# Attention with packed queries and a two-layer MLP on one Trainium2 core: two more block-product groups, crossbar transposes of queries, idle matmuls, another order

## The chip, the cores and the metric

The kernel runs on one core of a Trainium2 chip. The core has a matrix engine (TensorE, PE in the profile, with its weight loads as PEld), a vector engine (VectorE, DVE), a scalar engine (ScalarE, ACT), GpSimd (POOL) and SyncE (SP). Each engine takes its instructions in order, and waits on semaphores where one needs the result of another. PE writes only to PSUM, from which DVE or ACT copy. DMAs are issued by SP, ACT or POOL and carried out by 16 shared DMA engines. The metric is device time in microseconds; the median of the runs counts.

## What is computed

`q`, `k`, `v` have shape (8, 8, 576, 64): eight batches of eight heads with 576 tokens of 64 numbers. `p` has 32 packed queries for each head. The reference, cut to what matters:

```python
def sm_attn(qq, kk, vv):
    s = scale * np.matmul(qq, kk.transpose(0, 1, 3, 2))       # scale = 1/8
    a = np.exp(s - np.max(s, axis=-1, keepdims=True))
    a = a / (np.sum(a, axis=-1, keepdims=True) + 1e-09)
    return np.matmul(a, vv)
p_packed = sm_attn(p, k, v)            # 32 rows per head
out = sm_attn(q, p_packed, p_packed)   # 576 rows per head, over 32 keys
x = out.transpose(0, 2, 1, 3).reshape(4608, 512)
h = x @ w_in                           # 512 -> 2048
g = np.maximum(h, 0) ** 2
return g @ w_out                       # 2048 -> 512
```

All inputs and the output are float32; the kernel computes in bfloat16 with sums in float32.

## The kernel before

**Tiling.** Work goes by batch. The heads form two quads `qd` of four. For a batch `b`: `tr_k` transposes the keys in 32x32 blocks on DVE, `s1` (L283, L296) multiplies them with the block-diagonal packed queries, `s1_exp` takes the exponential, and `pv` (L316, L320) multiplies with `v` and sums. `extract` copies the result `pp` to SBUF, `recip` takes the reciprocal of the sums, and `pq_block` (L331, casts at L164 and L166) writes `pp` once more as a block-diagonal matrix `pq_bd`. `m` (L354) multiplies `pp` with `w_in` before attention is applied, as 64x32 tiles of the array: the product `M` has 32 rows for each head, 256 in all. `tr_q` (L267) transposes the queries on DVE into the single tile `qT`. `s2` (L379) multiplies `qT` with `pq_bd`, `s2_exp` (L386) takes the exponential, `n_sum`, `n_ln`, `n_inv` and `n_mul` (L391, L396, L399, L405) normalise. `f1_mm` (L417) then multiplies the attention weights with `M`: a piece `fb` of 128 of the 2048 hidden columns is four matmuls of 288 columns into a tile of `ps_h` (two exist). `f1_relu` (L445 on ACT, L447 on DVE) and `f1_sq` (L452, DVE) make the columns of `gT`. Batch 0 (in `SPLIT`) is done in halves (L426, L435, L437); all others are "wide".

**Layer two.** The 4608 tokens are 36 tiles of 128. A tile alone is 16 matmuls of 512 columns (`f2_mm`, L501) into one of the two banks `ps_o` (tiles 2 and 3: `ps_a`), one copy into `o_sb` (three buffers) and a store. Four tiles from each number in `GROUPS` are computed together with seven block products in place of eight (Strassen's scheme in Winograd's form): `w_sum` (L525) makes four sums of blocks of `w_out` once, `g_sum` (L546) makes four sums `wS` of blocks of `gT` for each group in two halves each, `prod` (L560) runs seven products of 16 matmuls of 256 columns, and `prod_out` (L166 or L164, and L573 where it adds) empties a bank after each product, so seven times instead of four. The last tile, 35, is done in two halves of 256 columns (L487).

**Stores.** `store` (L477) issues four DMAs of 32 rows for a tile at the point where its last copy is emitted, all on SP; for the last tile two of each four go to ACT.

**Order.** The schedule is written by hand, with no reordering: each step is cut into pieces with the engines that may do it and a planned time, and `ORDER` (L71) is a compressed list that names, for each piece, its engine and its position. `Plan.run` (L59) emits the pieces in that sequence, and each engine keeps the order in which it got them. The planned times, the number of buffers (`plan.nslots`, L585) and `plan.base` (L859), the planned starting times of engines and DMA, are used for making the list only. Loads are issued by POOL (they convert float32 to bfloat16), at most eight under way (`dl`); the keys of batch 0 come in float32 on SP and ACT (L221).

Of the kernel before, what the change touches and what calls it, by code (L numbers as in the profile page):

```python
# [14 lines left out]
P = 128  # L15
D = 64
NP = 32
QH = 4
# [8 lines left out]
GROUPS = (15, 19, 23, 27, 31)  # L27
SPLIT = (0,)

# [20 lines left out]
class Plan:  # L50

    def __init__(self, slots):
        self.nslots = slots
        self.streams, self.base = [], {}

# [3 lines left out]
    def run(self, order):  # L59
# [5 lines left out]
        for c, p in sorted(zip(code, pieces), key=lambda x: x[0] % 4096):  # L65
            e, us, fn = p.alts[c // 4096]
            self.log.append((p.step.name, p.stage, e, c % 4096, us))
            fn()


ORDER = (  # L71
    'c-jrtgMu9i6a~Pm)5-X86x+6K+qP}nwr$(CZQHhY>nn=LD1aOaqU01vp_H0J$V=%+DJCT*AH}2W<fbUfL>Vb7m7*+^n<`Km%0R^^0VSb=RFq0n'
    'Z7NUIsSCBDj<k@PP#c;-J!v3qp%FBJ4p2>ML_?`QHK*|un-Wr9s!Fw}FO{T<)Qmb%H(E<$X)>LpO|*-i(rQ{y_h=f;p-VKMmeDmjLZ|30U8L)z'
    'e4NhGce+iF$i)xo1;yg$^qvy&JNiN?`78aQtn6VQ7v}_=ge&nsiou20&vCdMXW;BymuqnYp2&H*2)E&;+@4o(DXzdhcmNOQZJdnLaCI)vRk<&Z'
    '<;i@Et8r}}%p-Ul@8w3^lIQSO{>KqAgBS35e!_3~7x(1;ypeqpTT)A2DJ12@CE=1lp7Td0DJJEmp%j$jQd@5E1Afi-`6++m(o#j5$$S3JK~hm_'
    'N_)wm*|mVqmnE`JmdkqCD>=2G*4DMMSq{r$StVQLtNanuESg)(YcVaWEwr3g*S`8spniQI&*ZKA6jqm((n{J%^J#Idr%a$=5{f~Q6o=xw;!;vd'
    'Mk!pmD2!a>p<a}O^3XT>O&z!kAL6UrPiDz=xh=!J<21EpF+YX7V!0wH+BJZ7l5sm0xg>2h5v8I6RD{Y=6{<sHD3lX&J}%4McnR;|ef)z>Qc5<d'
    'ERE!{ypteJuA_9C&eq+U&dOLNTW={TEv2Vyl$ml;KFUvpsIaRHm7wCTQ8bmN&`g?5i|H>3$K(Ka1c$hzxD40eDqN2nb2IMB6L>05<3&81=eh6j'
    'W4^~<_$UA2K=DYVM0v7ELQgz7BuC|l9GBB_R<6iZxhZ!%ujRQslv-L>8)-9btZlTNcGND~%{xMSX>adKeXXzboxayk`dPp0PyOX(3o`PxvbNUF'
    '23kk!W<zYajk57J)28?q`dU&uS9=;p6KOQ<pna}AbeV3@eR8vx<8omx%@z3(zu=edzwAh`#FylfUXIC0&jqQY4ZIDtwYK+m&^|iAJ5WFB7yasO'  # L80
    'W4)|{4YFZ2#-`aUo8x<9@9e#=ELEmTRE=s-U1~^8sU9_^*3_9APz!2Hov15yr+ze;dQfi~LL(_LC*@R}meX+-F2Kb&8|UJpT$$JKdfvcWcsuXr'
    'yX=)~e1ln%NDj#@`K72-kgC#Fx=I)6E(2t!e3EbSTSx;mSUnm`!!$zUX(1h><8`b~)~PyEm*`5JrE_(g9#gMHSbR%jnJt^;vG$hF3Ro$tVH<6;'
    '?Xcap#}3*l`)Nn)m_4u%^r1o2pN7*on&g^J^Jp$DaxJBmw1zg&M%qe8=>#34b98~OxbDysdPcA54Sl4~^pk#(<F3OE-SxSJyDfL(&fJ}QaUbr-'
    'LwFdE<}o~pr|?Xk#mjgxujV~`fDiH!KF+83G@s)Oe3=VNS*a!Uq=7V%rqV*%NGItjeWb4p@(hvTGDgP9B$?`&BGYA_ERqGXLe|Je*(BR!r|gzJ'
    'vR`h=eYq!3<f*)rSMpx|N=)@?Y>lf4yzw=OH<_l?)S6b)X(r94xipU!)}mTk%V=etuM2gNF7+<gRk~W&=?2}bTXeg3r|!|cx?d0K5k0CW^pu{}'
    'b9zxP=~ca^H}$sO*9ZDYpXv+!r|J`PEWm;-(84U-Vq08GV96|vrLv5c--=pED{G~#f>pMvR?TW!ZL4SXt&uIYRleo6+D_VeyI_~?s@<@gcE|49'
    'Q~P1R?U(&C0pK7ef)I)@xZy_x!V%?9h$KjiWd4*$gS5ziOvs9C$ca42k3uMl;wXjED2Ixuf*Poe`e=nlXo~jegpTOr?~Y!WMayYB9j3eViilJ2'
    'Kpx5Cc`a|^GklS6b8G1(qh*53mDRFC4$5cwB|c5BS+%5A)S9|hH|Zfgt(Wz>KGx^zw|JJ&3R)d&Xw9s(U9^Yx+7yBCA|BEqI|`!&YN91NqX&jz'
    '0j;9Vw3|-T8G1=S2pq_f9FLQ8PR`E-xu$ysZKJ)kpAOM2`aqv3h=Vyc$LHLfhf8otZp}+*9UY|ebd_$>1A0u%VI0oUoSM^fCeF+`+)cPSx8jc6'
    'n+New9>vpnF3;zMyp&h+X5Pgo+!^^HXOIF?L`q3rSt$4PjegKS>b7W0ZaJ*8^|Qe?)F#?=TV~sApB=UncFk_tJxhel$c-|njJjxuCYXX*Sb}xf'  # L90
# [13 lines left out]
def kernel_impl(tc, q, k, v, p, w_in, w_out, out):  # L104
# [15 lines left out]
    with ExitStack() as ctx:  # L120
# [38 lines left out]
        def bd(t, h, dh):  # L159
            return both(t, dh * BDW + 32 * h, P + (-32 if h % 2 else 32), 32)[32 * h:32 * h + 32]  # L160
# [524 lines left out]
        def s2_steps(b):  # L685
# [16 lines left out]
            if wide:  # L702
                return [res[0], res[2], res[1], res[3]]
# [228 lines left out]
```

The softmax here doesn't subtract the row's maximum and nothing guards it: scores larger than these inputs give would overflow.

## Time and profile before

| | |
|---|---|
| five runs | 251.13 us median, 249.48 to 252.84 |
| profiled execution | 251.13 us, its span 249.1 us |
| mean granted PE clock | 0.988 |
| matmuls start, end | 7.7 us, about 241.7 us |
| matmuls L501 / L560 / L417 | 240 / 560 / 448 |
| DVE transposes of q (L267) | 18, 21.9 us together |
| HBM read, written | 37.22 MB, 9.44 MB |

The page cuts the span into 40 slices of 6.2 us each. A digit is the busy share in tenths:

```profile
DVE  4875649876788797679787989988897798768410
ACT  3377667985697676776788788887875756400010
POOL 7797556562075003261010000000000000000000
PEclk9999999999799999999999999999999999999997
DMA  6999999999969963799711010033004101504243
GB/s 222 202 183 204 205 201 208 204 246 218 180 79 185 247 137 57 118 167 213 143 45 42 3 42 3 0 75 99 3 21 118 34 3 39 130 2 105 66 108 103
```

Loads fill the DMA engines in the first ten slices and come in lumps until slice 20; what follows is mostly stores. The clock row shows one slice below full, between 62 and 68 us, and the last. In tables of groups a row gives line, engine, operation, output<-inputs, shape and count, busy time and mean duration, then the idle time of the engine just before, with what ended it. In a timeline a row starts with start and length in us; the lengths of matmuls are modelled and overlap, so the pace is read from start to start.

### The profile page before, as it was taken

To read this page: it belongs to the slowest core of one execution; us is meant where nothing else is said; L and a number is where in the kernel's file an instruction comes from. 1 tells how busy PE (TensorE), PEld (TensorE's weight loads), DVE (VectorE), ACT (ScalarE), POOL (GpSimd) and SP (SyncE) were. 2 spreads that over 40 slices of the span, in tenths; PEclk is the share of its full clock that TensorE was granted. 3 is DMA by queue.
4 is the path that set the end of the run, shared out by engine and by line. 5 is a ranking of instruction groups with operands and counts; after the bars stand their busy time and mean duration, and the time that the engine had idled before them with its cause. 6 is when DMAs were issued, how large, how long until landed. Compare 5 with 4: busy or idle time off the path is not lost.

```text
span 249.1 us, 5373 instructions
## 1 busy us (share of the span) xinstructions
PE 227.8 (91%) x2096; PEld 161.3 (65%) x2096; DVE 186.0 (75%) x325; ACT 157.8 (63%) x273; POOL 59.9 (24%) x120
## 2 busy tenths in 40 slices
PE   0669999996999999999999999999999999999980
PEld 0525564573554666666646778887787888888860
DVE  4875649876788797679787989988897798768410
ACT  3377667985697676776788788887875756400010
POOL 7797556562075003261010000000000000000000
PEclk9999999999799999999999999999999999999997
DMA  6999999999969963799711010033004101504243
GB/s 222 202 183 204 205 201 208 204 246 218 180 79 185 247 137 57 118 167 213 143 45 42 3 42 3 0 75 99 3 21 118 34 3 39 130 2 105 66 108 103
DMA packets 27160, 29.01 MB, mean 116 GB/s; under 512 B 5760, under 2 KB 18816, under 8 KB 27136
## 3 DMA queue, kind: packets, MB, share of 16 engines
q0 software_dynamic: 19472, 17.99, 45.6%
q1 hardware_dynamic: 7328, 9.97, 14.7%
q10 hardware_dynamic: 336, 0.72, 0.8%
q8 instruction: 16, 0.26, 0.4%
q14 instruction: 8, 0.07, 0.1%
HBM read 37.22 MB, written 9.44 MB: 187 GB/s over the span
## 4 chain that ended last, share of the span: by engine, by line
PE 70%; DMA 19%; POOL 4%; issue 2%; DVE 1%; SPq 0%; ACT 0%; POOLq 0%
PE ps_o L560 24%; PE ps_h L417 20%; PE ps_o L501 15%; DMA v_r<-in_v_dram 6%; DMA w_in_b<-in_moe_w_in_dram 4%; DMA q_b<-in_q_dram 4%; DMA k_b<-in_k_dram 4%; PE ps_m L354 3%; PE ps_s L379 2%; PE ps_a L283 2%; PE ps_pp L316 1%; PE ps_s L391 1%; DMA out_dram<-o_sb 1%; POOL w_in_b L246 1%; POOL v_r L238 1%
## 5 line engine op out<-in xcount | busy, mean ns | idle before, releaser
L445 ACT ACTIVATE r<-ps_h 128x576 bf16<-128x576 f32 x99 | 63.7, 650 | 27.5 <-PE ps_h L417 25.5
L417 PE MATMUL ps_h<-a,M 128*128 128x288 bf16 x448 | 71.6, 288 | 0.0
L501 PE MATMUL ps_o<-w_out_b,gT 128*128 128x512 bf16 x208 | 59.2, 382 | 0.5 <-DMA w_out_b<-in_moe_w_out_dram 0.5
L417 PEld LDWEIGHTS <-M 128*128 128x128 bf16 x448 | 43.9, 98 | 16.8 <-issue 0.5
L452 DVE TENSOR_TENSOR gT<-r 128x1152 bf16<-128x1152 bf16 x64 | 46.9, 747 | 7.6 <-ACT r L445 5.5
L560 PEld LDWEIGHTS <-wS 128*128 128x128 bf16 x320 | 31.0, 98 | 4.7 <-issue 0.4
L501 PEld LDWEIGHTS <-gT 128*128 128x128 bf16 x240 | 22.6, 99 | 17.0 <-issue 3.4
L560 PE MATMUL ps_o<-wT,wS 128*128 128x256 bf16 x240 | 30.5, 273 | 0.0
L238 POOL DMA_DIRECT2D v_r<-in_v_dram x32 | 19.0, 598 | 35.3 <-DVE wT L525 16.3
L164 ACT CAST M<-ps_m 128x1024 bf16<-128x1024 f32 (+1 forms) x26 | 23.0, 915 | 5.8 <-PE ps_m L354 4.9
L267 DVE STREAM_TRANSPOSE qT<-q_b 128x1152 bf16<-128x1152 bf16 (+1 forms) x18 | 21.9, 1227 | 5.5 <-DMA q_b<-in_q_dram 5.4
L560 PEld LDWEIGHTS <-gT 128*128 128x128 bf16 x240 | 23.3, 98 | 3.8 <-issue 0.4
L164 ACT COPY o_sb<-ps_o 128x512 f32<-128x512 f32 (+1 forms) x15 | 8.6, 572 | 22.7 <-PE ps_o L560 19.6
L560 PE MATMUL ps_o<-w_out_b,gT 128*128 128x256 bf16 x160 | 20.9, 273 | 0.0
L166 DVE COPY o_sb<-ps_o 128x512 f32<-128x512 f32 (+1 forms) x20 | 13.4, 671 | 8.1 <-PE ps_o L560 3.6
L283 PE MATMUL ps_a<-pT_bd,kT 128*128 128x128 bf16 x128 | 10.9, 241 | 8.2 <-DVE kT L273 8.2
L386 ACT ACTIVATE e<-ps_s,rD 128x576 bf16<-128x576 f32 (+1 forms) x18 | 12.2, 687 | 8.0 <-PE ps_s L379 8.0
L166 DVE CAST M<-ps_m 128x1024 bf16<-128x1024 f32 (+1 forms) x10 | 11.2, 1118 | 6.8 <-PE ps_m L354 6.1
L283 PEld LDWEIGHTS <-kT 128*128 128x128 bf16 x128 | 9.2, 109 | 10.8 <-DVE kT L273 8.7
L573 DVE TENSOR_TENSOR o_sb<-ps_o,o_sb 128x512 f32<-128x512 f32 x15 | 10.3, 689 | 6.2 <-PE ps_o L560 5.0
L379 PE MATMUL ps_s<-qT,pq_bd 128*128 128x288 bf16 x64 | 11.6, 306 | 3.3 <-DVE qT L267 2.0
L405 DVE SCALAR_TENSOR_TENSOR a<-e,rD,ls 128x576 bf16<-128x576 bf16 (+1 forms) x18 | 13.3, 740 | 1.5 <-ACT ls L399 1.5
(72 smaller groups left out, 303.7 us busy)
## 6 DMA issues: line engine op xcount, KB each, us to landing
out_dram<-o_sb SPq DMA_DIRECT2D x140, 64.0 KB, 1.7
k_b<-in_k_dram POOLq DMA_DIRECT2D x14, 288.0 KB, 8.7
q_b<-in_q_dram POOLq DMA_DIRECT2D x14, 288.0 KB, 8.7
v_r<-in_v_dram POOLq DMA_DIRECT2D x16, 160.0 KB, 8.5
v_r<-in_v_dram POOLq DMA_DIRECT2D x16, 128.0 KB, 6.9
w_in_b<-in_moe_w_in_dram POOLq DMA_DIRECT2D x8, 256.0 KB, 8.9
w_out_b<-in_moe_w_out_dram POOLq DMA_DIRECT2D x8, 256.0 KB, 8.5
k_f<-in_k_dram ACTq DMA_DIRECT2D x1, 576.0 KB, 4.2
```

What stands on the lines that cost most here:

```text
L164: nc.scalar.copy(dst, src)
L166: eng.tensor_copy(dst, src)
L238: nc.gpsimd.dma_start(self.vr[32 * i:32 * i + 32, h0:h1, :n * D], src[:, :, J0[i] * D:(J0[i] + n) * D])
L267: nc.vector.transpose(self.qT[:, qd, :, j0 * 32:j1 * 32].rearrange("p dh (j a) -> p j dh a", a=32), self.t.qb[qd][:, j0 * D:j1 * D].rearra ...
L283: nc.tensor.matmul(ps[:, g * P:(g + 1) * P], lhsT=self.kT[:, qd, g * P:(g + 1) * P].bitcast(BF16).rearrange("p (t two) -> p two t", two=2) ...
L379: nc.tensor.matmul(ps[:, c], lhsT=self.pq[:, blk(qd, dh)], rhs=self.qT[:, qd, dh, n0:n0 + HALF], start=(dh == 0), stop=(dh == 1))
L405: nc.vector.scalar_tensor_tensor(out=self.a2[:, qd, n0:n1].rearrange("p (c n) -> p c n", n=HALF), in0=self.e2[qd, hf], scalar=self.rD[:, q ...
L417: nc.tensor.matmul(ps[:, c, :HALF], lhsT=a.M[:, qd, fb * FB:(fb + 1) * FB], rhs=a.a2[:, qd, c * HALF:(c + 1) * HALF], start=(qd == 0), sto ...
L445: nc.scalar.activation(dst, src, ACT.Relu)
L452: eng.tensor_tensor(out=gT[:, fb - 1:fb + 1, o:o + S], in0=r, in1=r, op=ALU.mult)
L501: nc.tensor.matmul(po[t], lhsT=gT[:, fb, n0:n0 + P], rhs=w_out_b[:, fb, :], start=(fb == 0), stop=(fb == NFB - 1))
L560: nc.tensor.matmul(ps[:, u * EH:(u + 1) * EH], lhsT=lhs, rhs=rhs, start=(n in (1, 2, 4) and kk == 0 and u == 0), stop=(kk == KB - 1 and u ...
```

## The change

- `GROUPS` gets 7 and 11: tiles 7 to 14 are computed as block products too, seven groups in all.
- `XBAR` names batches 4 to 7. Their `q` is transposed by a DMA issued by SP (`xbar_q`, SBUF to SBUF) instead of by DVE. Pairs of token columns lie in the partitions then, so the rows of those batches come out in another order, and `store` addresses them accordingly. `qT` has two buffers instead of one.
- The block-diagonal `pq_bd` and its two memsets fall away. `s2` runs as small tiles of the array instead: 32 matmuls of 32x32 for a wide batch (16 for each half of batch 0), or 16 matmuls of 64x32 for a batch in `XBAR` (`s2_x`), both quads in one step, which takes both `ps_h` tiles. `pq_part` copies the blocks that lie in the wrong partitions (three small casts in each of two pieces), `pq_swap` does it in two casts for batches in `XBAR`.
- `FILL` and `keep_clock`: ahead of eleven early steps PE runs 97 matmuls in all, of 224 columns, of a zeroed tile; their result is overwritten.
- `f1_sq` may run on ACT; `e1` and `e1r` have one buffer; `e2` has two for each quad instead of three in all.
- Stores are steps of their own, in pieces of two DMAs, on SP, on POOL (from tile 8 on) or on ACT (from tile 31 on).
- `ORDER` is another list, some planned times differ, and `setup_rest` on POOL is shorter by one memset.

The diff, without the list and with less of the planning:

```diff
-GROUPS = (15, 19, 23, 27, 31)
+GROUPS = (7, 11, 15, 19, 23, 27, 31)
 SPLIT = (0,)
+XBAR = (4, 5, 6, 7)
+PQ_PARTS = (((0, 1), (1, 0), (1, 1)), ((2, 0), (2, 1), (3, 0)))
...
+            self.fill = FILL.get(p.step.name, 0) if e == "PE" else 0
...
+FILL = {'S1.0.0': 31, 'S1.0.1': 4, 'PV.0.0': 12, 'M.0.0': 16, 'N.0.0.0': 11, 'S2.0.1': 3, 'N.0.0.1': 10, 'R.0.0': 1, 'R.0.2': 3, 'R.0.1': 4, 'R.0.4': 2}
...
+            nc.vector.memset(idle_b, 0.0)
...
-            nc.vector.memset(pq_bd[0][:, :BDW + 2 * P], 0.0)
...
-            nc.gpsimd.memset(pq_bd[1][:, :BDW + 2 * P], 0.0)
+
+        def keep_clock(ps):
+            for _ in range(plan.fill):
+                nc.tensor.matmul(ps, lhsT=idle_b[:, :P], rhs=idle_b, start=True, stop=True)
...
             def tr_q(self, qd, hf=None):
-                self.tile_of("qT", att, [P, NQD, 2, S], BF16, bufs=1)
+                self.tile_of("qT", att, [P, NQD, 2, S], BF16)
...
+            def xbar_q(self, qd):
+                self.tile_of("qT", att, [P, NQD, 2, S], BF16)
+                nc.sync.dma_start_transpose(self.qT[:, qd].rearrange("p dh s -> p (dh s)").rearrange("p (jp r) -> p jp r", r=P), self.t.qb[qd])
...
             def s1(self, qd):
                 ps = ps_att.tile([P, 512], F32, name="ps_a", tag="a")
+                keep_clock(ps[:, :224])
...
-            def pq_block(self, pr, eng):
+            def pq_part(self, i, eng):
+                self.tile_of("pq", small, [P, NQD, 2, 32], BF16, bufs=2)
                 ps = self.ps_pp if eng is nc.vector else self.pp
-                for e in range(2):
-                    for dh in range(2):
-                        s0 = 64 * e + 32 * dh
-                        cast(eng, bd(self.pq, 2 * pr + e, dh),
-                             both(ps, pr * 64 + 32 * e, P + (-32 if e else 32), 32)[s0:s0 + 32])
+                for h, dh in PQ_PARTS[i]:
+                    pr, e = divmod(h, 2)
+                    s0 = 64 * e + 32 * dh
+                    cast(eng, self.pq[32 * h:32 * h + 32, :, dh], both(ps, pr * 64 + 32 * e, P + (-32 if e else 32), 32)[s0:s0 + 32])
+
+            def pq_swap(self, e, eng):
+                self.tile_of("pq", small, [P, NQD, 2, 32], BF16, bufs=2)
+                ps = self.ps_pp if eng is nc.vector else self.pp
+                s = P + (-32 if e else 32)
+                src = ps[64 * e:64 * e + 64, 32 * e:32 * e + 2 * s].rearrange("p (q c i) -> p q c i", q=2, i=32)[:, :, 0:3:2]
+                cast(eng, self.pq[64 * (1 - e):64 * (1 - e) + 64], src)
+
+            def packed(self, h, qd, dh):
+                pr, e = divmod(h, 2)
+                if e + dh == 2 * pr:
+                    return self.pp[32 * h:32 * h + 32, qd * P + pr * 64 + 32 * (e ^ qd):][:, :32]
+                return self.pq[32 * h:32 * h + 32, qd, dh]
...
-            def s2(self, qd, hf):
-                ps = self.pss[qd, hf] = self.ps_s(hf)
+            def s2_x(self):
+                for qd in range(NQD):
+                    ps = self.pss[qd, None] = ps_h.tile([P, 2, 512], F32, name="ps_s", tag="h")[:, :, :HALF]
+                    qT = self.qT[:, qd].rearrange("p dh s -> p (dh s)").rearrange("p (jp r) -> p jp r", r=P)
+                    for x in range(QH):
+                        h = x ^ qd
+                        pr, e = divmod(h, 2)
+                        for par in range(2):
+                            w = self.pp[:, qd * P + pr * 64 + 32 * (x % 2):][:, :32] if par == e else self.pq[:, qd, pr]
+                            nc.tensor.matmul(ps[32 * x:32 * x + 32, par].rearrange("p (jp a) -> p jp a", a=32), lhsT=w[64 * par:64 * par + 64],
+                                             rhs=qT[64 * par:64 * par + 64, :, 32 * h:32 * h + 32], start=True, stop=True)
+
+            def s2(self, hf):
+                if self.b in XBAR:
+                    return self.s2_x()
+                if hf is None:
+                    pss = [ps_h.tile([P, 2, 512], F32, name="ps_s", tag="h")[:, :, :HALF] for _ in range(NQD)]
+                else:
+                    ps = ps_h.tile([P, 2, 512], F32, name="ps_s", tag="h")
+                    keep_clock(ps[:, 0, :224])
+                    pss = [ps[:, qd:qd + 1, :HALF] for qd in range(NQD)]
                 for c, n0 in enumerate([hf * HALF] if hf is not None else [0, HALF]):
                     for dh in range(2):
-                        nc.tensor.matmul(ps[:, c], lhsT=self.pq[:, blk(qd, dh)],
-                                         rhs=self.qT[:, qd, dh, n0:n0 + HALF],
-                                         start=(dh == 0), stop=(dh == 1))
+                        for h in range(QH):
+                            for qd in range(NQD):
+                                o = 32 * (h ^ qd)
+                                nc.tensor.matmul(pss[qd][o:o + 32, c], lhsT=self.packed(h, qd, dh), rhs=self.qT[32 * h:32 * h + 32, qd, dh, n0:n0 + HALF],
+                                                 start=(dh == 0), stop=(dh == 1))
+                for qd in range(NQD):
+                    self.pss[qd, hf] = pss[qd]
...
-            eng.tensor_tensor(out=gT[:, fb - 1:fb + 1, o:o + S], in0=r, in1=r, op=ALU.mult)
-
-        po, ob = {}, {}
+            dst = gT[:, fb - 1:fb + 1, o:o + S]
+            if eng is nc.scalar:
+                eng.activation(dst, r, ACT.Square)
+            else:
+                eng.tensor_tensor(out=dst, in0=r, in1=r, op=ALU.mult)
...
-        def store(t, src, eng=None, e0=0, e1=NE):
-            for i in range(4):
+        def store(t, src, i0, eng, e0=0, e1=NE):
+            for i in range(i0, i0 + 2):
                 b, j = divmod(t * 4 + i, JT)
+                if b in XBAR:
+                    j = 2 * (j % JH) + j // JH
                 dst = out[b * S:(b + 1) * S, e0:e1].rearrange("(a j) e -> j a e", j=JT)[j]
-                (eng or nc.sync if i % 2 else nc.sync).dma_start(dst, src[32 * i:32 * i + 32])
+                eng.dma_start(dst, src[32 * i:32 * i + 32])
...
-                old = [f"S2.{b - 1}.{qd}.{hf}" for qd, hf in halves(b - 1)]
+                old = [f"S2.{b - 2}.{hf}" for hf in parts(b - 2)] if b > 1 else []
             us = 0.84 if nm == "k" else 1.37
+            if nm == "q" and b in XBAR:
+                return [Step(f"Tq.{b}.{qd}", [stage([("SP", 0.4, lambda qd=qd: T[b].xbar_q(qd))]), stage([("-", 1.2, lambda: None)]),
+                                              stage([("DMA", 2.0, lambda: None)])],
+                             [f"Lq.{b}.{qd}"] + old, (), [("kqb", 2, f"Lq.{b}.{qd}")], lag=0.5) for qd in QDS]
...
+                res.append(Step(f"S2.{b}.{hf}",
+                                [stage([("PE", (0.25 if b else 0.5) * m, lambda hf=hf: T[b].s2(hf))]),
+                                 stage(*[[("ACT", 0.73 if wide else 0.49, lambda qd=qd, hf=hf: T[b].s2_exp(qd, hf))] for qd in QDS])],
+                                [f"XT.{b}/2.{i}" for i in range(3)] + [f"Tq.{b}.{qd}" + (f".{hf}" if b in SPLIT else "") for qd in QDS],
+                                [("h", m), ("e20", 1), ("e21", 1)], [("h", 1, None)]))
...
-                res.append(Step(f"F1.{b}.{fb}", [stage([("DVE", 0.77, lambda fb=fb: f1_sq(T[b], fb, V))])], deps, (),
+                res.append(Step(f"F1.{b}.{fb}", [stage([("DVE", 0.77, lambda fb=fb: f1_sq(T[b], fb, V)), ("ACT", 1.14, lambda fb=fb: f1_sq(T[b], fb, A))])], deps, (),
...
+        def store_step(name, ts, after, slot, hf=None):
+            def piece(t, i):
+                args = (hf * EH, (hf + 1) * EH) if hf is not None else ()
+                return [(e, us, lambda eng=eng: store(t, src[t if hf is None else (t, hf)], i, eng, *args))
+                        for e, us, eng in (("SP", 0.86, nc.sync), ("POOL", 1.0, Q), ("ACT", 0.86, A))
+                        if e == "SP" or t >= (8 if e == "POOL" else 31)]
+            return Step(f"ST.{name}", [stage([("-", 0.0, lambda: None)]), stage(*[piece(t, i) for t in ts for i in (0, 2)]),
+                                       stage([("-", 1.8, lambda: None)])],
+                        [after], (), [("osb", 2, slot)] if slot else [], lag=0.1)
...
-        plan.base.update(DVE=2.7, POOL=1.25, ACT=2.1, ACTQ=0.75, SP=0.7, DMA=1.85, PE=3.6)
+        plan.base.update(DVE=2.5, POOL=1.25, ACT=2.1, ACTQ=0.75, SP=0.7, DMA=3.2, PE=3.6)
...
+        plan.stream(7.5, store_steps())
```

## The prediction

> **What bounds the kernel now.** I read the page first, then windows, then the groups of TensorE (PE) instructions after the last stall, then timelines of the places where PE does not run at full pace, and the stores at the end.
>
> ```profile
> PE 227.8 (91%) x2096; PEld 161.3 (65%) x2096; DVE 186.0 (75%) x325; ACT 157.8 (63%) x273; POOL 59.9 (24%) x120
> ...
> 80.00:140.00 60.00, 60.00 (x502) 37.17 (x501) 48.87 (x82) 44.16 (x72) 11.34 (x24) 1.00 0.66 125
> ...
> 150.00:190.00 40.00, 40.00 (x421) 33.02 (x416) 35.90 (x65) 31.45 (x58) 0.00 (x0) 1.00 0.17 41
> ```
>
> The two window rows give length, then busy us of PE, weight loads, DVE, ACT and POOL, the clock, the DMA share and GB/s. PE has no recorded idle time. Since ends of matmuls are modelled, I counted: the groups after 65.4 us, each at its pace from start to start (0.49 us for 4 matmuls of 288 columns, 0.216 for one of 512, 20.32/186 = 0.109 for one of 256, 0.56 for 16 packed ones), give some 174.5 us of work. The last matmul ends near 241.7, so 176.3 us pass. PE is 99% full for seven tenths of the span: there a microsecond of PE work removed is a microsecond gained, as long as DVE and ACT keep up. They are 82% and 74% busy in 80 to 140, 90% and 79% in 150 to 190.
>
> The places where PE loses time lie before and after that stretch:
>
> ```profile
> 7.69 1.04 PE L283 MATMUL ps_a<-pT_bd,kT 128*128 128x128 bf16 x8 [7.69 <-DVE kT L273]
> ...
> 13.48 1.15 PE L379 MATMUL ps_s<-qT,pq_bd 128*128 128x288 bf16 x4 [1.26 <-ACT pq_bd L164]
> ...
> 47.42 0.61 PE L283 MATMUL ps_a<-pT_bd,kT 128*128 128x128 bf16 x8
> ...
> 59.28 0.38 PE L501 MATMUL ps_o<-w_out_b,gT 128*128 128x512 bf16 x1
> 61.70 0.78 PE L379 MATMUL ps_s<-qT,pq_bd 128*128 128x288 bf16 x4 [2.04 <-DVE qT L267]
> ```
>
> The same eight matmuls of L283 take 1.04 us at 7.69 and 0.61 at 47.42. Until about 24 us everything on PE goes at half pace, though the granted clock of the early slices reads full. At 59.7 PE stands 2.04 us, because the queries of batch 2 landed at 60.24, and then it runs at half clock again: the windows 60 to 65 and 65 to 70 have a mean granted clock of 0.71 and 0.95, which is some 3.4 us at 0.5 and costs 1.7 us more.
>
> ```profile
> 236.00:241.70 5.70, 5.65 (x52) 4.81 (x50) 1.12 (x2) 0.58 (x1) 0.00 (x0) 1.00 0.37 98
> 241.70:249.10 7.40, 0.00 (x0) 0.00 (x0) 0.00 (x0) 0.37 (x1) 0.00 (x0) 0.82 0.39 102
> ...
> L481 SPq DMA_DIRECT2D out_dram<-o_sb x20: 314/421/435, 237.2 to 246.5; - x20
> L481 ACTq DMA_DIRECT2D out_dram<-o_sb x4: 322/389/462, 240.4 to 242.5; - x4
> ```
>
> After the last matmul 7.4 us pass, with one copy of 0.37 us in them. SP issues stores one after another at 0.42 us from 237.2 until 246.5, while ACT's last is issued at 242.5. The end is a backlog of SP's queue.
>
> **The change, part by part.** I sum against the profiled run (251.13 us, span 249.07), which is also the median of the five.
>
> *Two more product groups* (tiles 7 to 14). A group of four tiles is 64 matmuls of L501 or 112 of L560: 64 x 0.216 = 13.8 against 112 x 0.109 = 12.2 us. Twice 1.6 is **-3.2**. On DVE each adds a fifth of the wS work of five groups, (13.6+6.8+6.8)/5 = 5.4 us, and three more evictions at 0.69: 7.5 a group, 15 in all. Eight transposes of 1.37 us leave DVE (-11 in all, some 5.5 before 140) and the block-diagonal casts shrink (from eight of about 0.23 a batch to six, or two larger ones planned at 0.3; about -1 a batch). In 80 to 140 that is 48.9 + 15 - 5.5, over 58 of 60 us. ACT must take some of it: the diff lets it square (planned at 1.14 us, against 0.747 on DVE), and it has 16 us free there. DVE at 90% with ACT at 79% left PE full in 150 to 190; the sum here, (58.4+44.2)/120 = 85%, is the same, but less even. I charge **+3** (0 to +10).
>
> *Packed scores.* S2 was eight matmuls a wide batch, 2 x 0.49 = 0.98 us. Now batches 4 to 7 use 16 on tiles of 64 rows by 32 columns, the others 32 on 32 by 32. The nearest row is the product M:
>
> ```profile
> 73.22 0.41 PE L354 MATMUL ps_m<-w_in_b,pp 64*32 64x512 bf16 x8
> ...
> 73.45 0.40 PE L354 MATMUL ps_m<-w_in_b,pp 64*32 64x512 bf16 x8
> 73.78 0.39 PE L501 MATMUL ps_o<-w_out_b,gT 128*128 128x512 bf16 x1
> ```
>
> Eight run together, eight more 0.23 us later, the next work at 0.56: two rounds of 0.216 and some 0.12 for entering and leaving. So 16 matmuls of 288 columns cost 2 x 0.122 + 0.12 = 0.36 (-0.62), 32 cost 4 x 0.122 + 0.12 = 0.61 (-0.37). A rule speaks against it: the Trainium skill, TensorEngine Tiling (Array Packing), Gotcha 1: PSUM Pressure, says that different row tiles cannot use one PSUM bank at the same time. In the 32-row form four row tiles write one bank; by the rule they go in turn, 16 x 0.122 = 1.95 us, +1.0 a batch instead of -0.37. But in the row above the two row tiles of M write the same bank and start together, so I go by the row; by the rule the sum would be 1.3 us worse, since only batch 3 of that form lies in the full stretch (the 64-row form puts its two row tiles in two banks). A batch's scores now take both ps_h tiles at once, as M does already; F1 then waits for one exp (L386, 0.69 us), which layer-two matmuls cover; without them 0.7 a batch, 3.5 in all. Batches 3 to 7: **-2.9** (+1 to -2.9; a dearer issue of four row tiles, which no row shows, would eat the gain).
>
> *Queries through the crossbar.* Eight transposes of 288 KB on SP's queue. The trace shows none. Nearest rows: a 64 KB store lands in 1.7 us, a 288 KB load among other loads in 8.7; 261 GB/s with a split middle dimension, as the skill has it (DMA: Bandwidth & Descriptors, Latency and other measured facts), would be an estimate of 1.1 us and the latency. I take 4 us each, 1.7 to 9 as the ends. They are hidden: the DVE transposes they replace were done at 85 to 88 (batch 4), 111 to 117 and 132 to 140, and the scores that use them began at 108, 130 and 154, at least 13 us after. Batch 7's second transpose at 179.7 was just in time, but its q was issued at 117.6, and qT now has two buffers. Cost 0. What stands behind a waiting transpose on SP is stores, and behind them three o_sb buffers, then PSUM; SP waits for data most of the time (99 us on one line of its waits), and DMA is a fifth busy after 120.
>
> *Idle matmuls.* 97 of 224 columns. The 31 ahead of the first S1 can start after a first memset, near 1.3 us: 18 at half pace (0.187) and 13 at full (0.093) end near 6, before kT is there at 7.69. The other 66 are 6.1 us at full pace; PE's idle time in 10 to 20 is 2.8 us and grows by the half-pace time saved there, so they fit barely. Half-pace work until 24 us adds up to some 11 us, so at most 5.5 is to be had. From 20 to 59 PE has hardly a gap, so what is won can be carried on, unless weights (landing until 43) hold it: **-3.0** (+4 to -5.5).
>
> *Another order.* The stop at 59.7 to 65.5 cost 3.75 us. The plan now takes loads to land 1.35 us later than it did (DMA base 1.85 to 3.2), so it will put other work into most of it: tiles 4 to 6 are ready by then, as F1 of batch 1 ended at 57.8. **-2.5** (+3, where another step meets its data late, to -3.75). POOL's memset of 0.64 us goes; it stands among load issues, but DMA is full there: 0.
>
> *Stores* become steps of their own, two DMAs each, spread over SP and POOL, for the last tile ACT too. 16 issues of the last group at 0.42 in two queues are out by about 241. Then copy 0.37, two issues 0.84, landing 1.7 from the last issue, and the 0.9 between landing and end as now: 3.5 after the last matmul instead of 7.4. POOL's issues of loads took 0.56 and land slower, so **-3.5** (0 to -3.9).
>
> Sum: -3.2 + 3.0 - 2.9 + 0 - 3.0 - 2.5 - 3.5 = -12.1: **239.0 us**.
>
> **The rivals.**
> *Early gains don't last (B).* Until 61 us loads keep DMA full (205 GB/s in nearly every slice), and their order stays. If the q of batch 2 still decides, a PE that is early only waits longer: the two parts of -5.5 fall away, 244.5. For it: the DMA row; against it: work of tiles 4 to 6 was lying there.
> *DVE becomes the bound in 80 to 140 (C).* Friction of 9 to 12 instead of 3, most of the rest kept: about 248.
> *The clock doesn't answer to idle matmuls (F).* They do not do what they are for: 66 x 0.187 = 12.3 us against gaps of 3 to 8 puts 4 or more onto PE where 3 were to be won: 246.
> *Slower: the crossbar (D).* At S2 of batches 4 to 7 PE's queue waits in order. The pair of a batch has at least 13 us; beyond that each microsecond stops PE four times. The other gains, about 12, are gone when a pair takes 16 us, 8 a transpose; slower by 1% from 17. At 9 us each, the upper end above, 4 x (18-13) = 20 makes 259. Against it: loads of this size need that long only when DMA is full, which it is not after 120.
>
> **How the numbers follow.** Forecast 0.48 (239), B 0.21 (244.5), C 0.12 (248, half of it within 1%), F 0.07 (246), D 0.12 (259). Faster by over 1% (under 248.6; less than that can't be told from no change): 0.48 + 0.21 + 0.07 + 0.06 = 0.82; within 1% 0.06; slower 0.12. The low end takes every gain at its full size and no friction, -19: 232. With B, C and F the range reaches 250; outside lie D, a little of C and of the forecast's low end, under 0.2.
>
> **What would show it.** L283's first group at about 0.6 us; no gap over 1 us and no half clock near 60; L501 at 112 matmuls and L560 at 784; 16 packed score matmuls in under 0.4 us; DVE under 95% in 80 to 140; 3 to 4 us from the last matmul to the end, no SP row past it by 5. I am wrong if PE waits for a DMA-written qT, if PE shows gaps in the middle stretch with DVE as releaser, or if the idle matmuls stand ahead of work whose data are there.

## The result, and the profile after

| | |
|---|---|
| forecast | 239.0 us (232 to 250) |
| before | 250.47 us median of 80 runs |
| after | 248.71 us median of 43 runs, 246.64 to 251.96 |
| ratio after / before | 0.9923, 95% interval 0.9905 to 0.9941 |

The change brings 1.8 to 1.9 us where 12.1 were forecast. Ratios here leave disturbed runs out; medians don't, so the two can differ a little. The profile shown is that of a repeat of the changed kernel (label after_again, 247.92 us, span 246.2); the first one (label after) is of an execution of 250.35 us, above the median, and is used only where it is named. Line numbers of the changed kernel: S1 L296 and L310, packed scores L430 (32x32) and L413 (64x32), idle matmuls L192, F1 L470, a tile alone L561, group products L620, last tile L547, casts and copies L170 (ACT) and L172 (DVE), stores L541. In experiments that add lines of code they are 2 to 9 higher.

The page, and windows in the columns of before (length, then busy us of PE, weight loads, DVE, ACT, POOL, clock, DMA share, GB/s); the last is from the last matmul to the end:

```profile
PE 226.8 (92%) x2407; PEld 173.7 (71%) x2417; DVE 181.1 (74%) x315; ACT 159.0 (65%) x265; POOL 89.0 (36%) x177
...
POOL 8765476618482012094603300240016005004070
PEclk9799999999999999999999999999999999999995
```

```profile
80.00:140.00 60.00, 56.28 (x637) 44.62 (x635) 47.66 (x79) 46.05 (x73) 19.39 (x39) 1.00 0.75 128
150.00:190.00 40.00, 40.00 (x429) 33.00 (x414) 33.05 (x54) 29.39 (x46) 8.25 (x17) 1.00 0.19 49
237.80:246.20 8.40, 0.00 (x0) 0.00 (x0) 0.00 (x0) 0.37 (x1) 0.95 (x2) 0.67 0.17 47
```

PE had 60.00 busy us of 60 in 80 to 140 and now has 56.28: it stands 3.7 us there, while DVE, at 47.66, is no busier than before. The last matmul ends at 237.8 instead of 241.7, so PE is 3.9 us early; but 8.4 us pass after it where 7.4 did. The half clock near 62 to 68 is gone from the clock row, and one slice below full lies at the start, from 6.2 to 12.3 us. POOL, idle after 125 us in before, has stores in slices up to the last but one.

The start of PE's timeline, and later the packed scores:

```profile
1.05 5.09 PE L192 MATMUL ps_a<-idle_b 128*128 128x224 bf16 x31 [1.05 <-DVE idle_b L175]
8.09 0.69 PE L296 MATMUL ps_a<-pT_bd,kT 128*128 128x128 bf16 x8 [1.95 <-DVE kT L285]
...
11.32 1.59 PE L192 MATMUL ps_pp<-idle_b 128*128 128x224 bf16 x12 [0.47 <-ACT e1r L317]
12.74 0.28 PE L331 MATMUL ps_pp<-e,v_b 128*128 128x64 bf16 x4
...
43.93 0.29 PE L430 MATMUL ps_s<-qT,pp 32*32 32x288 bf16 x2
...
44.54 0.82 PE L561 MATMUL ps_o<-w_out_b,gT 128*128 128x512 bf16 x2
```

The first S1 takes 0.69 us instead of 1.04: the 31 idle matmuls do raise the pace, though in this profile not for long; the second S1, at 9.39, takes 1.03 us again. But 12 more stand ahead of PV, whose data were there at 11.32, and PV begins 1.4 us later. The 32 packed score matmuls pass in 0.61 us (43.93 to 44.54), as forecast.

The end: each engine's store instructions after 225 us (minimum, median, maximum ns; first and last start), and the rows of the program's last line:

```profile
L541 POOL DMA_DIRECT2D out_dram<-o_sb x10: 496/496/498, 233.6 to 238.3; - x10
L541 SPq DMA_DIRECT2D out_dram<-o_sb x8: 314/420/617, 224.7 to 238.6; - x8
L541 ACTq DMA_DIRECT2D out_dram<-o_sb x8: 321/407/566, 233.3 to 238.6; - x8
```

```profile
L1024 POOLq DRAIN  x3: 46/97/7283, 238.1 to 245.9; - x3
L1024 SPq DRAIN  x3: 7/7/13, 241.5 to 245.6; - x3
```

SP's backlog is gone: its last store is issued at 238.6, not 246.5. What stands in its place is one DRAIN of 7283 ns on POOL's queue. It starts at 238.1, while POOL's last store is being issued (until 238.8), and ends at 245.4, 0.8 us before the span does. The drains of the other queues take 7 ns to 2.2 us, and the longest of them, PE's, is over when the last matmul is.

### The profile page after: what moved, and what is told of

Read it like the earlier page. It is cut to its first block, busy times and chain, and to the rows that moved or that the text cites. A ratio compares the mean times of both kernels' runs of the same rounds, so it can differ in the third digit from the quotient of the medians.

```text
span 248.5 us, 6016 instructions
## 1 busy us (share of the span) xinstructions
PE 227.7 (92%) x2417; PEld 173.3 (70%) x2417; DVE 181.3 (73%) x315; ACT 158.8 (64%) x265; POOL 90.1 (36%) x177
## 3 DMA queue, kind: packets, MB, share of 16 engines
q10 hardware_dynamic: 528, 1.05, 1.4%
## 4 chain that ended last, share of the span: by engine, by line
PE 60%; DMA 24%; DVE 5%; POOL 4%; issue 2%; ACT 1%; POOLq 0%; DVEq 0%
PE ps_o L620 29%; PE ps_h L470 17%; DMA v_r<-in_v_dram 12%; DMA w_in_b<-in_moe_w_in_dram 7%; DMA q_b<-in_q_dram 5%; PE ps_a L561 3%; PE ps_o L561 3%; PE ps_m L383 3%; PE ps_pp L331 1%; DVE v_b L172 1%; PE ps_a L296 1%; POOL out_dram L541 1%; PE ps_s L444 1%; DVE gT L510 1%; PE ps_s L413 1%
## 5 line engine op out<-in xcount | busy, mean ns | idle before, releaser
L470 PE MATMUL ps_h<-a,M 128*128 128x288 bf16 x448 | 71.8, 286 | 1.7 <-DVE r L501 1.7
L541 POOL DMA_DIRECT2D out_dram<-o_sb x58 | 28.7, 502 | 102.8 <-DVE o_sb L633 92.0
L470 PEld LDWEIGHTS <-M 128*128 128x128 bf16 x448 | 43.7, 98 | 12.8 <-issue 2.3
L620 PEld LDWEIGHTS <-wS 128*128 128x128 bf16 x448 | 42.6, 98 | 9.3 <-issue 3.2
L620 PE MATMUL ps_o<-wT,wS 128*128 128x256 bf16 x336 | 41.7, 273 | 0.4 <-DVE wS L606 0.4
L620 PEld LDWEIGHTS <-gT 128*128 128x128 bf16 x336 | 32.7, 98 | 5.6 <-issue 0.2
L620 PE MATMUL ps_o<-w_out_b,gT 128*128 128x256 bf16 x224 | 32.5, 273 | 0.0
L170 ACT COPY o_sb<-ps_o 128x512 f32<-128x512 f32 (+1 forms) x24 | 13.8, 575 | 24.7 <-PE ps_o L620 21.1
L170 ACT CAST M<-ps_m 128x1024 bf16<-128x1024 f32 (+1 forms) x26 | 23.5, 931 | 2.0 <-PE ps_m L383 1.8
L561 PE MATMUL ps_o<-w_out_b,gT 128*128 128x512 bf16 x80 | 23.1, 380 | 0.1
L606 DVE TENSOR_TENSOR wS<-gT 128x1024 bf16<-128x1024 bf16 (+1 forms) x32 | 19.1, 617 | 0.2
L561 PEld LDWEIGHTS <-gT 128*128 128x128 bf16 x112 | 10.1, 98 | 10.3 <-issue 2.0
L620 PE MATMUL ps_o<-wT,gT 128*128 128x256 bf16 x112 | 16.3, 273 | 0.0
L620 PE MATMUL ps_o<-w_out_b,wS 128*128 128x256 bf16 x112 | 15.8, 273 | 0.0
L501 DVE TENSOR_SCALAR r<-ps_h 128x576 bf16<-128x576 f32 x15 | 11.3, 756 | 5.9 <-PE ps_h L470 5.9
L192 PEld LDWEIGHTS <-idle_b 128*128 128x128 bf16 x97 | 10.7, 114 | 5.8 <-issue 3.6
```

The lines of the kernel that those rows point to most:

```text
L170: nc.scalar.copy(dst, src)
L470: nc.tensor.matmul(ps[:, c, :HALF], lhsT=a.M[:, qd, fb * FB:(fb + 1) * FB], rhs=a.a2[:, qd, c * HALF:(c + 1) * HALF], start=(qd == 0), sto ...
L541: eng.dma_start(dst, src[32 * i:32 * i + 32])
L561: nc.tensor.matmul(po[t], lhsT=gT[:, fb, n0:n0 + P], rhs=w_out_b[:, fb, :], start=(fb == 0), stop=(fb == NFB - 1))
L606: eng.tensor_tensor(out=dst, in0=a, in1=b, op=op)
L620: nc.tensor.matmul(ps[:, u * EH:(u + 1) * EH], lhsT=lhs, rhs=rhs, start=(n in (1, 2, 4) and kk == 0 and u == 0), stop=(kk == KB - 1 and u ...
```

## The experiments

Three suspects came from the comparison: GpSimd's drain at the end, the two stops of PE in 80 to 130, the idle matmuls. Each was first undone alone (the first four experiments). These four were timed beside the kernel before, but not beside the changed kernel; their ratios are to be compared with its 0.9923 with care. The four from before_tail to after_again were timed together, and so were the last four.

**Late stores off GpSimd** (tail_off_pool)

```diff
+        def other(name, t, i):
+            if str(name)[:2] in ("31", "35"):
+                return A if (t + i // 2) % 2 else nc.sync
+            return Q
-                        for e, us, eng in (("SP", 0.86, nc.sync), ("POOL", 1.0, Q), ("ACT", 0.86, A))
+                        for e, us, eng in (("SP", 0.86, nc.sync), ("POOL", 1.0, other(name, t, i)), ("ACT", 0.86, A))
```

> The changed kernel; only the stores of the last group (tiles 31 to 34) and of tile 35 that POOL issued are issued by SP and ACT in turn. Theory (drain): POOL's queue closes with a drain of 7.28 us after its last store, and that sets the end; the last stores have landed 6 us before it. Then the drain ends early, the time from the last matmul to the end falls from 8.4 to 4 us, and the kernel is 4 us faster: 0.976 of before instead of 0.992. Rival (landing): the end waits for stores, whoever issues them; then 0.990 to 0.994. Second rival: the drain is paid for POOL having issued so many DMAs at all, whenever; then it stays at 7 us and nothing changes.

Measured: 0.9858 (0.9799 to 0.9917), from three runs of six; the other three took 249.8 to 250.0 us, and with them the median is 248.93, so the ratio by itself shows little. The profiled span is 243.8. Its drain:

```profile
L1029 POOLq DRAIN  x3: 46/98/6463, 224.0 to 243.5; - x3
```

With 48 stores of POOL instead of 58 the drain is 6463 ns, and it begins near 224, where matmuls cover it: 4.8 us follow the last matmul instead of 8.4. So a drain is still paid, as the second rival has it, but it no longer shows. The gain is smaller than it could be, since a store on ACT stood ahead of ACT's copy, and PE waited 1.39 us for that copy at 237.14.

**Early group stores off GpSimd, so that its loads come sooner** (loads_first): the same edit with `name in ("7.6", "7.7", "11.6", "11.7")` and `nc.sync`.

> The changed kernel; only the stores of groups 7 and 11 that POOL issued are issued by SP. Theory (stores ahead of loads): from 97 to 106.75 us POOL waits for o_sb with a store, and the loads of v behind it land at 126 instead of some 9 us earlier; PE's stop of 2.0 us at 125 and its neighbours go, 2 to 2.5 us in all: 0.983 of before. Rival (slots): the loads wait for free buffers or for DMA anyway, and issue no earlier than 105: 0.992.

Measured: 0.9851 (0.9813 to 0.9889), span 244.6. The load of v for batch 6 still waits until 105.8, for its buffers, and the cast of v at 123.8 still waits 2.5 us. So POOL's queue does not hold v up. Yet the ratio is below the rival's 0.992. Part of that is the drain, with 42 stores instead of 58:

```profile
L1029 POOLq DRAIN  x3: 46/97/5970, 237.8 to 244.3; - x3
```

It is 1.3 us shorter, and 7.1 us follow the last matmul instead of 8.4.

**Casts of v later in DVE's order** (casts_later): three steps get a later place in the list, those of batch 4 and the first of batch 6.

```diff
+MOVE = {('Cv.4.0', 0, 0): 650.3, ('Cv.4.1', 0, 0): 650.4, ('Cv.6.0', 0, 0): 929.5}
-        for c, p in sorted(zip(code, pieces), key=lambda x: x[0] % 4096):
+        for c, p in sorted(zip(code, pieces), key=lambda x: MOVE.get((x[1].step.name, x[1].stage, x[1].k), x[0] % 4096)):
```

> The changed kernel; only the casts of v of batch 4 stand two squares and a relu later in DVE's order, and the first one of batch 6 behind the extraction of batch 5. Loads are as late as before. Theory (order on DVE): what stops PE at 86 (1.7 us) and at 125 (2.0 us) is not v, which PE needs later, but the relu and the extraction that stand behind the waiting cast on DVE. Then both stops go and PE ends 3 to 4 us earlier: 0.978. Rival (v itself is late): PE stops a little later for PV or S1 instead, and at most 1 us is won: 0.989 to 0.992.

Measured: 0.9841 (0.9793 to 0.9888), span 244.4. Timeline of the two places in the changed kernel:

```profile
82.60 0.49 DVE L172 COPY v_b<-v_r 128x1280 bf16<-128x1280 bf16 x1 [1.92 <-DMA v_r<-in_v_dram]
...
84.75 0.75 DVE L501 TENSOR_SCALAR r<-ps_h 128x576 bf16<-128x576 f32 x1
...
85.55 0.65 PE L470 MATMUL ps_h<-a,M 128*128 128x288 bf16 x4 [0.48 <-DVE r L501]
...
120.94 0.16 PE L335 MATMUL ps_pp<-ones_c,e1r 128*128 128x1 bf16 x1
...
124.06 0.49 DVE L172 COPY v_b<-v_r 128x1280 bf16<-128x1280 bf16 x1 [3.57 <-DMA v_r<-in_v_dram]
124.47 0.41 DVE L172 CAST pp<-ps_pp 128x256 bf16<-128x256 f32 x1
...
124.94 0.29 PE L413 MATMUL ps_s<-qT,pp 64*32 64x288 bf16 x1 [2.06 <-DVE pp L172]
```

and with the casts moved:

```profile
84.46 0.76 DVE L503 TENSOR_SCALAR r<-ps_h 128x576 bf16<-128x576 f32 x1 [0.20 <-PE ps_h L472]
...
86.00 0.89 DVE L174 COPY v_b<-v_r 128x1280 bf16<-128x1280 bf16 x2
...
121.00 0.42 DVE L174 CAST pp<-ps_pp 128x256 bf16<-128x256 f32 x1 [0.65 <-PE ps_pp L337]
```

The stop at 85.55 is 0.48 us here, and was 1.67 in the first profile. At 124 the row to read is not PE's but the one above it. PE waits for pp, whose sums were ready at 121 (the row at 120.94 is the last of them); DVE had pp queued behind a cast that waited 3.57 us for a load. Moved, the copy of pp starts at 121.00 instead of 124.47. PE's window 120 to 130, in the changed kernel and with the casts moved:

```profile
120.00:130.00 10.00, 7.91 (x103) 6.46 (x103) 5.72 (x13) 6.07 (x10) 2.60 (x7) 1.00 0.60 106
...
120.00:130.00 10.00, 9.32 (x118) 7.63 (x116) 7.33 (x16) 7.28 (x12) 2.45 (x7) 1.00 0.62 109
```

PE ends 1.7 us earlier, between the theory's 3 to 4 and the rival's 1.

**Idle matmuls only ahead of S1** (fill_s1_only)

```diff
+FILL = {'S1.0.0': 31, 'S1.0.1': 4}
```

> The changed kernel; only the 35 idle matmuls ahead of the two S1 of batch 0 stay, the other 62 go. Theory (in the way): those after S1 wait for the same PSUM tile as the step behind them, so they start when the step could and delay it by their length (1.15 us at PV, 1.05 at N, and so on): work done by 40 us rises from 17.7 to 19 or 20 us. If PE is full from there to 80, some 1 to 2 us arrive at the end (0.985); if loads decide, nothing does (0.992). Rival (clock): without them the clock falls back in the gaps, early matmuls run at half pace again, and the kernel is slower by 1 us or more (0.996 to 1.0).

Measured: 0.9848 (0.9808 to 0.9889), span 245.1. The granted clock falls, as the rival says, from 0.91 to 0.82 in 0 to 20 and from 1.00 to 0.92 in 20 to 40, but the kernel is not slower. Work done by 40 us, counted by groups at their full pace, is 19.3 us against 17.8, as the theory asks; how little of that the idle matmuls explain is seen in c_fill_all below, which has all of them and 18.8.

**Spreading without GpSimd, on the kernel before** (before_tail)

```diff
-                (eng or nc.sync if i % 2 else nc.sync).dma_start(dst, src[32 * i:32 * i + 32])
+                ((nc.scalar if i % 2 else nc.sync) if t >= 31 else nc.sync).dma_start(dst, src[32 * i:32 * i + 32])
```

> The kernel before with only one edit: the stores of tiles 31 to 35, which SP issued alone there, go to SP and ScalarE in turn; no store goes to GpSimd. The prediction gave the spreading of the late stores -3.5 us, and the changed kernel showed about +1 because its three queues include GpSimd, whose drain stands at the end. Theory (the spreading itself is worth what was forecast, GpSimd's drain ate it): the span ends about 3.5 us after the last matmul instead of 7.3, ratio to before 0.984 to 0.988. Rival (SP's backlog was hidden by landing time, or ScalarE's issuing delays its copies as much as it saves): 0.994 to 1.003.

Measured: 0.9888 (0.9838 to 0.9938), 247.73 against 249.79 us, span 245.5. The last matmul ends at 241.0 and 4.5 us follow, where 7.4 did and 3.5 were expected. The spreading is worth 2.1 to 2.8 us by itself; the forecast of 3.5 was a little high.

**Crossbar transposes of batch 4 issued later** (xbar4_later): `MOVE` with 'Tq.4.0' and 'Tq.4.1' at 623.3 and 623.4.

> The changed kernel, with SP's issue of batch 4's two crossbar transposes moved behind the stores of tiles 5 and 6, some 8 us later. Theory of contention (the 256-byte packets of the transposes lengthen the loads of v for batch 4, whose landing 10.65 us after issue holds VectorE's cast at 85): that load lands in 6 us or less, VectorE's wait for v_r at 85 (3.1 us) falls below 1 us and TensorE's stretch 80 to 90 rises from 8.3 us busy to above 9; ratio to before about 0.985. Rival (the load is long by its own size and by the other loads, as the cast's place in VectorE's order and the buffer slots set it): landing still 9 us or more, the wait of 2.5 us or more stays, ratio within 0.003 of the changed kernel's in this call.

Measured: 0.9852 (0.9799 to 0.9904), where the changed kernel timed beside it has 0.9934. The cast of v came at 82.13 instead of 82.60, and its wait fell from 1.92 to 1.45 us, not below 1 as the theory asks; the load still lands late. The stretch 80 to 90 has 9.51 busy us, as the theory asks, but the changed kernel had 9.03 in after_again already. Its window 120 to 130 has 8.64 us against 7.91, which moved transposes of batch 4 do not explain; without this edit that window has 7.51 to 8.91 in five profiles. So the ratio fits the theory and the trace for the most part the rival. On the changed kernel this stays open; c_xbar_later below asks again with the casts moved.

The five edits that were tried alone on the changed kernel lie between 0.9841 and 0.9858, with intervals that overlap, and the theories of two of them (loads_first, xbar4_later) were not borne out by their traces. One ratio can't tell these causes apart. The traces do. A stop of PE of over 1 us that ends with DVE's pp stands near 124 to 127 in all six profiles of the change with its casts in place (1.05 to 2.06 us), and in none of the six with the casts moved. After the last matmul 7.1 to 8.4 us pass in every kernel that stores late on GpSimd, and 4.5 to 5.5 in the experiments that don't, except c_fill_all (7.1), where SP waited for a store.

**The three together** (combined): GpSimd's late stores all to SP, casts moved, idle matmuls only ahead of S1.

> The changed kernel with three edits that were tried one by one: the stores of the last two groups of tiles leave GpSimd, this time all for SP so that ScalarE's copies have no store ahead of them; the casts of v of batches 4 and 6 stand later in VectorE's order; idle matmuls only ahead of the first two S1 steps. If the three causes are independent (drain about 2.5 to 3.5 us at the end, casts about 1.5, idle matmuls about 1), the sum is 5 to 6 us under the changed kernel: ratio to before 0.968 to 0.975, a span near 240. If the gains of the middle are eaten at the end (the last groups wait for something else, such as SP's own backlog or the early loads' landing), 0.982 to 0.988, no better than any of the three alone.

Measured: 0.9655 (0.9608 to 0.9702), 242.17 us, span 239.6. Better than both kernels, and about what the theory asked: the interval reaches into its range, the medians alone give 0.9695, and the span is near its 240.

```profile
80.00:140.00 60.00, 58.85 (x673) 47.18 (x679) 50.59 (x85) 47.75 (x77) 20.64 (x39) 1.00 0.82 140
...
234.20:239.60 5.40, 0.00 (x0) 0.00 (x0) 0.00 (x0) 0.36 (x1) 0.00 (x0) 0.96 0.34 90
```

Against the changed kernel PE has 2.6 us more in 80 to 140, its last matmul ends 3.6 us earlier, and 5.4 us follow instead of 8.4.

**The changed kernel again** (after_again)

> The changed kernel as it is, as the measure for the other three in this call: ratio to before 0.990 to 0.994 as measured, last matmul some 7 us before the span's end, with GpSimd's drain of about 7.3 us as the last row. If the drain comes from chance and not from the count and place of GpSimd's stores, it differs from 7.28 us by more than 0.3 us.

Measured: 0.9934 (0.9894 to 0.9974), drain 7283 ns against 7280 in the first profile: not chance.

**Four late DMAs back on GpSimd** (c_two_late): in `combined`, `other` returns `Q` for the step "35.0".

> The combined kernel with the first half of the last tile stored by GpSimd again, four of its DMAs, issued last but one; the other 48 of GpSimd's stores are as in the combined kernel. Theory (the drain at GpSimd's end grows with all its stores and begins after its last instruction): with 52 stores it is 6.5 + 4 x 0.082 = 6.8 us, begins at about 236 and ends at about 243: span 243 to 244.3 instead of 239.6, ratio to before 0.980 to 0.986. Rival (the drain of the changed kernel was long since ten or more stores came late, and a drain only waits for the stores still under way): four late stores add 1 us at most, ratio 0.965 to 0.970.

Measured: 0.9797 (0.9749 to 0.9845), 244.59 us, span 243.1.

```profile
L1033 POOLq DRAIN  x3: 46/98/6793, 235.5 to 242.8; - x3
```

POOL's last store ends at 236.2, the drain, begun at 235.5, takes the 6.8 us that were expected, and 7.9 us follow the last matmul instead of 5.4. Four DMAs in the wrong queue cost about 2.4 us, against combined (242.17) and against c_xbar_later (242.15), which was timed beside it. The rival's 1 us is ruled out.

**No idle matmuls, and all of them, on the combined kernel** (c_fill_none with `FILL = {}`, c_fill_all with the change's `FILL`)

> The combined kernel with no idle matmuls at all. Theory (those ahead of the first S1 steps speed up work on the path: S1 0.62 instead of 1.04 us and the steps up to 30 us at a higher clock): granted clock in 0 to 20 below 0.8, work done at 40 us 0.5 to 1.2 us less than 18.7, ratio to before 0.969 to 0.973. Rival (early work waits for loads and for the other engines, so that the clock is worth nothing): 0.963 to 0.967, as the combined kernel.

> The combined kernel with all 97 idle matmuls of the change. Theory (those of the later steps stand ahead of their step in the same PSUM tile and delay it by up to 1.15 us each time): clock 0.9 or more in 0 to 20, yet work done at 40 us 0.5 to 1 us less than the combined kernel's 18.7 and ratio to before 0.968 to 0.973. Rival (they cost nothing once the end has room, the better clock is worth as much as the delay): 0.963 to 0.967.

Measured: none 242.79 us, 0.9738 (0.9694 to 0.9782); all 244.08 us, 0.9788 (0.9753 to 0.9823). With none the granted clock reads 1.00 in 0 to 20, so that expectation missed, though S1 runs at half pace:

```profile
7.84 1.03 PE L298 MATMUL ps_a<-pT_bd,kT 128*128 128x128 bf16 x8 [7.84 <-DVE kT L287]
...
11.09 0.37 PE L333 MATMUL ps_pp<-e,v_b 128*128 128x64 bf16 x4 [0.47 <-ACT e1r L319]
...
13.61 0.77 PE L385 MATMUL ps_m<-w_in_b,pp 64*32 64x512 bf16 x8 [1.06 <-DVE pp L174]
...
19.34 1.12 PE L482 MATMUL ps_h<-a,M 128*128 128x288 bf16 x4
```

With all of them:

```profile
8.33 0.62 PE L298 MATMUL ps_a<-pT_bd,kT 128*128 128x128 bf16 x8 [1.78 <-DVE kT L287]
...
12.08 0.28 PE L333 MATMUL ps_pp<-e,v_b 128*128 128x64 bf16 x4
...
14.54 0.41 PE L385 MATMUL ps_m<-w_in_b,pp 64*32 64x512 bf16 x8
...
20.91 0.65 PE L482 MATMUL ps_h<-a,M 128*128 128x288 bf16 x4
```

At half pace the first F1 begins at 19.34, at full pace at 20.91. With none, five steps of that chain begin with a wait of 0.26 to 1.06 us for ACT or DVE, so PE's pace matters little, and idle matmuls that wait for the step's own PSUM tile come just when its data do. By 40 us the counted work is 19.0 us with none, 18.8 with all and 18.6 in combined: both theories, which asked for a loss of 0.5 us or more, missed. The two ratios' intervals overlap, and the medians are 1.3 us apart. Of the 2.2 us between the two spans the last matmul shows 0.5; the rest lies in SP's last 16 stores, which took 9.5 us to issue with all and 7.8 with none. In the longer one SP waited 2.4 us at one point for a store to land, and why that store was late stays open. Those ahead of S1 alone (combined, 242.17; c_xbar_later, 242.15, timed beside none) are worth at most 0.6, which these intervals don't resolve.

**Crossbar transposes later, on the combined kernel** (c_xbar_later)

> The combined kernel with SP's issue of batch 4's crossbar transposes behind the stores of tiles 5 and 6, as tried on the changed kernel. Theory (the transposes hold SP's queue for 7 us and so the output buffers, which costs the middle something of its own): TensorE's windows 80 to 100 gain 0.5 us or more and the ratio is 0.960 to 0.963. Rival (on the changed kernel they cost only through the load of v, half a microsecond sooner, and the moved casts have taken that away): 0.964 to 0.968, as the combined kernel.

Measured: 242.15 us, 0.9714 (0.9678 to 0.9751), windows 80 to 100 unchanged (9.51 and 9.77). By the medians it equals combined (242.17); the ratio lies higher, over the rival's range too, with other runs of the kernel before under it. Once the casts stand later, the place of the transposes gives nothing: the windows and the median fit the rival.

## Why the prediction was wrong

Spans fall by 2.9 us (249.1 to 246.2) between the two profiles where 12.1 were forecast, and both parts of the sum missed: PE was to be done 8.6 us earlier and is 3.9, the stretch after it was to shrink by 3.5 and grew by 1.0. The time came out near rival C's 248, but not by what C describes.

- **Stores, -3.5, measured +1.0: the largest miss.** The step "16 issues of the last group at 0.42 in two queues are out by about 241" held: the last stores of SP and ACT are issued at 238.6, 0.8 us behind the last matmul. What failed is the next one, "3.5 after the last matmul": it took GpSimd's queue for one more queue like SP's and put nothing behind POOL's last store, where a drain of 7.28 us stands. Without GpSimd 4.5 us follow (before_tail), so about 3.9 of the 8.4 are the drain's; the rest of the miss is a sum that was short (0.37, 0.84, 1.7 and 0.9 add to 3.8). The trace of before had a row for the drain, which I did not read because POOL was done at 125.8 and nothing showed it at the end:

```profile
L927 POOLq DRAIN  x3: 46/98/3102, 124.6 to 248.8; - x3
```

- **Idle matmuls, -3.0, measured about +0.5 (last matmul) to +1.3 (medians)**, all 97 against none on the combined kernel. The pace did rise, so rival F is wrong in its mechanism. The step that failed is "half-pace work until 24 us adds up to some 11 us, so at most 5.5 is to be had": it counted PE's work as if it were the path. S1 gains 0.4 us and PV still begins when ACT's e1r is there. The prediction's own last sentence, idle matmuls ahead of work whose data are there, is what happened at 11.32.
- **Friction in 80 to 140, +3.0, measured 3.7** us of PE standing, and 5.3 by the prediction's own way of counting: by groups and paces PE did 59.8 us of work in that stretch before and 54.5 after. The busy time hides the difference, since the ends of matmuls are modelled. The size was near by accident. DVE's forecast 58 of 60 us was 47.66, so rival C's bound never formed. The 15 us of the new groups did come there (10.6 of wS, 4.1 of adding copies), but transposes of q took 8.2 away instead of 5.5, and 8.6 us of wT sums, casts of M and relu stood elsewhere or on ACT. The stops come from casts of v that wait for loads with the relu and pp behind them in DVE's order; moving three casts gave back 1.9 of the 3.7 us (2.2 of the 5.3). The prediction had named the sign, gaps in the middle with DVE as releaser, but no such wait.
- **Another order, -2.5, measured about -3.** No stop at 60 and no half clock: PE's windows from 60 to 80 have 19.73 busy us at clock 1.00, against 18.30 at 0.91 in before, and 1.4 more plus some 1.7 of half clock is 3.1. Not undone by itself.
- **Packed scores, -2.9.** 0.61 us for 32 matmuls, and 0.37 to 0.38 for 16 (98.98 to 99.36 and 187.10 to 187.47): the predicted 0.61 and 0.36. The row, not the rule, was right: the Trainium skill, TensorEngine Tiling (Array Packing), Gotcha 1: PSUM Pressure, would have made it 1.95. Four row tiles of the 32-row form do write one bank here, each to its own 32 partitions. Over all eight batches score work falls from 7.8 to 3.9 us, counted by groups and paces, and by 2.8 in batches 3 to 7, which the prediction counted. Not undone by itself.
- **Product groups, -3.2.** Layer-two work counted the same way falls from 116.4 to 113.3, and PE is full in 150 to 190. Not undone by itself.
- **Crossbar, 0.** PE never waited for a transposed qT, and rival D had no part. Landing took 3.2 to 12.7 us (to 14.0 in the first profile), the longest beyond my upper end of 9; it was hidden all the same.

With friction as counted, the measured terms add to -3.1 + 5.3 - 3.9 + 0.9 - 3.1 + 1.0 = -2.9 (0.9 is the middle for the idle matmuls), which is what the spans show. To the tenth that is luck: the order, the scores and the groups were counted, not undone, and the last matmul of the same kernel ends at 240.1 in the first profile and at 237.8 in the repeat. With the three faults out, combined is 9.5 us under before by the spans and 7.6 by the medians, near the -9.1 that the prediction's sum gives without its idle matmuls.

## What to carry to other kernels

A store moved to another queue must be priced to that queue's very end: look for its DRAIN in the trace, even where it lies hidden now, and let GpSimd finish early. When PE waits for a vector engine, read what stood ahead of the awaited instruction in that engine's order; a small cast that waits for a load can hold up everything behind it. Speeding up an engine pays only where its own work, not the latency of its partners, ends each step. And when several single edits all seem to gain the same, compare what their traces share before crediting any of them.

## What the runs showed of the hardware

GpSimd's drain grew with its stores: 3102 to 3104 ns with none (its loads alone), 5970 with 42, 6463 to 6468 with 48 (begun at 221 to 224, under matmuls), 6793 with 52, 7277 to 7285 with 58, so some 82 ns for each store above 42. The clock row does not show the half pace of the start: it reads 1.00 with no idle matmuls while S1 takes 1.03 us. In combined, where PE was brought to full pace and then stood from 11.9 to 13.6, it does show what follows (window, length, PE, clock, DMA share, GB/s):

```profile
12.00:16.00 4.00, 1.43 (x25) 0.74 1.23 204
16.00:20.00 4.00, 3.02 (x24) 0.50 1.20 206
20.00:24.00 4.00, 3.54 (x21) 0.50 1.23 204
```

The clock fell although no gap of PE between two matmuls was longer than 1.7 us there, while the stop of 2.06 us before 124.94 in the changed kernel left it at 1.00 (the window 120 to 130 above). The length of one gap does not decide it. The Trainium skill, TensorE: Matmul & The Clock Gate, Part 1: The HAM clock gate, names an idle window of about 3.4 us for that; these rows ask for one that is only partly idle, or for a shorter one that a stop of 2.06 us can miss. Which of the two no run tells apart.
